# Moving a check flag's load and a branch within the tail of TensorE's product stream

## The chip, the cores and the metric

The kernel runs on one core of one Trainium2 chip. The metric is device time in microseconds (us), the median of several executions. A profile of one execution is shown beside it. Its span, from the first to the last recorded instruction, is about 1.8 us shorter than the time. Ratios are the mean time of one kernel's fast runs over the mean of the other's in the same rounds, so they are not quite the ratio of the medians that are quoted.

## The reference

The reference is attention over a sliding window of a key and value cache, with an input and an output projection, in bfloat16:

```python
B, Sq, D = 8, 32, 1024;  Hq, Hkv, Sk, Dh = 32, 4, 8192, 128
W = min(4096, max(256, Sk // 4))                     # 2048
q = (x @ wq).reshape(B, Sq, Hq, Dh).transpose(0, 2, 1, 3)
k = repeat(k_cache[:, :, Sk - W:, :], Hq // Hkv);  v = the same of v_cache
p = softmax(einsum("bhqd,bhkd->bhqk", q, k) * Dh ** -0.5)
out = einsum("bhqk,bhkd->bhqd", p, v).transpose(0, 2, 1, 3).reshape(B, Sq, Hq * Dh) @ wo
```

## The kernel before

The kernel takes the exponential without first subtracting the row's maximum. That is exact only while the row sums stay in range. So it counts, for each (batch, head group) unit, the rows whose reciprocal sum lies within two limits. If any count is below 128, it branches to a slow, exact fallback. All five engines load the flag into a register and branch. The flag is ready only near the end, so the branch stands in the middle of the last output projection: some products come before it, some after.

```python
            with tc.manual_schedule(engines=order):
                flagi = fast.tail_begin()
        safe = nc.values_load(flagi[0:1, 0:1], min_val=0, max_val=1)     # register load, all engines
        with tc.If(safe < 1, label="fallback"):
            ...                                       # exact attention and projection; clears open PSUM
        with tc.manual_schedule(engines=order):
            fast.tail_end()
    ...
    def tail_begin(self):
        self.pv_last()
        for p in self.after[:-2]: p()
        flagi = self.check_all()                      # count product, minimum, conversion
        for p in self.after[-2:]: p()                 # 4 products of 512 columns
        self.last = self.o_pieces(self.Hkv - 1, 1, (512, 256, 128, 128))
        for p in self.last[:3]: p()                   # a piece is two products (load weights, multiply)
        self.last[3](mm=True)                         # with it: 8 products of 512 columns
        return flagi
    def tail_end(self):
        self.last[3](mm=False)                        # VectorE evicts the 512 columns, DMA to out
        for p in self.last[4:]: p()                   # 8 products of 256, 8 and 8 of 128, each evicted
    def check_all(self):
        ...
        nc.tensor.matmul(cnt[0:1, 0:2 * ncol], lhsT=self.ones_c[:, :], rhs=self.ok[:, :, :], start=True, stop=True)
        low = ck.tile([1, 1], FP32, name="low")
        nc.vector.tensor_reduce(out=low[:, :], in_=cnt[0:1, 0:2 * ncol], op=ALU.min, axis=AX.X)
        flagi = ck.tile([1, 1], I32, name="flagi")
        nc.vector.tensor_scalar(out=flagi[:, :], in0=low[:, :], scalar1=float(P) - 0.5, scalar2=None, op0=ALU.is_ge)
        return flagi
```

Products are summed in PSUM, a memory made of banks. VectorE then *evicts* a group: it adds the sum of the earlier blocks and writes the result to a tile that a DMA copies to the output. The last block's column groups (512, 256, 128, 128) take turns in two PSUM banks. A group may therefore start only when the group two before it has been evicted.

Of the kernel before, what the change touches and what calls it, by code (L numbers as in the profile page):

```python
# [9 lines left out]
ALU = mybir.AluOpType  # L10
AX = mybir.AxisListType
BF16 = mybir.dt.bfloat16
FP32 = mybir.dt.float32
# [20 lines left out]
@with_exitstack  # L34
def kernel(
    ctx: ExitStack,
    tc: tile.TileContext,
    x: bass.AP,
    k_cache: bass.AP,
    v_cache: bass.AP,  # L40
    wq: bass.AP,
    wo: bass.AP,
    out: bass.AP,
):
    nc = tc.nc
    B, Sq, D = x.shape
    _, Hkv, Sk, Dh = k_cache.shape
    HD = wq.shape[1]
    Hq = HD // Dh
    W = min(4096, max(256, Sk // 4))  # L50
    rep = Hq // Hkv
    scale = float(Dh) ** -0.5
    P = 128
    assert Dh == P and D % P == 0 and W % P == 0
    UQ = rep * Sq
    QT_N = UQ // P
    NU = B * Hkv
    out_flat = out.rearrange("b s d -> (b s) d")

    const = ctx.enter_context(tc.tile_pool(name="const", bufs=1))  # L60
    ident = const.tile([P, P], BF16, name="ident")
    make_identity(nc, ident[:, :])
    QT = [const.tile([P, B * UQ], BF16, name=f"QT{g}") for g in range(Hkv)]
    RL_all = const.tile([P, NU * QT_N], FP32, name="RL_all")

    E = mybir.EngineType
    order = {E.PE, E.SP, E.Pool, E.Activation, E.DVE}
    with ExitStack() as long_ctx:
        with ExitStack() as fctx:
            fast = Fast(tc, long_ctx, fctx, x, k_cache, v_cache, wq, wo, out_flat, QT, RL_all, ident)  # L70
            with tc.manual_schedule(engines=order):
                fast.run()
            hint_branch(tc, (E.PE,))
            with tc.manual_schedule(engines=order):
                flagi = fast.tail_begin()
        safe = nc.values_load(flagi[0:1, 0:1], min_val=0, max_val=1)

        with tc.If(safe < 1, label="fallback"):  # L78
            with ExitStack() as ectx:
                eo = ectx.enter_context(tc.tile_pool(name="e_ot", bufs=1))  # L80
                OT_e = eo.tile([P, NU * UQ], BF16, name="OT_e")
                Q_e = eo.tile([P, NU * UQ], BF16, name="Q_e")
                for g in range(Hkv):
                    nc.vector.tensor_copy(out=Q_e[:, g * B * UQ:(g + 1) * B * UQ], in_=QT[g][:, :])
                attention_exact(tc, k_cache, v_cache, Q_e, OT_e, B=B, Hkv=Hkv, Hq=Hq, Sq=Sq, Sk=Sk, W=W, Dh=Dh, scale=scale)
                out_proj(tc, wo, OT_e, out_flat, fast, Hkv=Hkv, Hq=Hq, Sq=Sq, NQ=B * Sq, D=D)

        with tc.manual_schedule(engines=order):
            fast.tail_end()
# [13 lines left out]
class Fast:  # L103
# [4 lines left out]
    def __init__(self, tc, long_ctx, ctx, x, k_cache, v_cache, wq, wo, out_flat, QT, RL_all, ident):  # L108
        self.tc, self.nc, self.ctx = tc, tc.nc, ctx
        self.x, self.k_cache, self.v_cache, self.wq, self.wo, self.out = x, k_cache, v_cache, wq, wo, out_flat  # L110
        self.QT, self.RL_all, self.ident = QT, RL_all, ident
        self.P = P = 128
        self.B, self.Sq, self.D = x.shape
        _, self.Hkv, self.Sk, self.Dh = k_cache.shape
        self.Hq = wq.shape[1] // self.Dh
        self.rep = self.Hq // self.Hkv
        self.W = min(4096, max(256, self.Sk // 4))
        self.NQ = self.B * self.Sq
        self.NT, self.DC, self.KT = self.NQ // P, self.D // P, self.W // P
        self.UQ = self.rep * self.Sq  # L120
        self.QT_N = self.UQ // P
        self.scale = float(self.Dh) ** -0.5
        self.units = [(b, g) for g in range(self.Hkv) for b in range(self.B)]
        self.CJ = 4
        self.NCH = self.KT // self.CJ
        self.VW = self.Dh + 1

        def pool(name, bufs, ctx=ctx, **kw):
            return ctx.enter_context(tc.tile_pool(name=name, bufs=bufs, **kw))

        self.c1 = pool("c1", 1, long_ctx)
        self.wp = pool("wp", 6, long_ctx)
        self.osb = pool("osb", 5, long_ctx)
        self.ps_m = pool("ps_m", 2, long_ctx, space=PSUM)
        self.krp = pool("krp", 4)
        self.kbp = pool("kbp", 2)
        self.kvt = pool("kvt", 2)
        self.ktp = pool("ktp", 5)
        self.vp = pool("vp", 6)
        self.ptp = pool("ptp", 5)  # L140
        self.ob = pool("ob", 2)
        self.ps_s = pool("ps_s", 2, space=PSUM)
        self.ps_o = pool("ps_o", 2, space=PSUM)
        self.OT = self.c1.tile([P, self.Hkv * self.QT_N, 4, self.NQ], BF16, name="OT")
        self.oacc = self.c1.tile([P, self.NT, self.D], FP32, name="oacc")
        self.ok = self.c1.tile([P, 2, len(self.units) * self.QT_N], BF16, name="ok")
        self.ones_c = self.c1.tile([P, 1], BF16, name="ones_c")
        self.xT = self.c1.tile([P, self.DC, self.NQ], BF16, name="xT")
        self.va = [self.c1.tile([P, self.KT, VA_ROW], BF16, name=f"va{i}") for i in range(3)]
        self.wq_t, self.wo_t, self.kT, self.v_sb, self.k_raw = {}, {}, {}, {}, {}  # L150
# [129 lines left out]
    def o_pieces(self, g, t, cuts=(512, 512)):  # L280

        nc, P = self.nc, self.P
        st = {}
        last = g == self.Hkv - 1

        def piece(n0, w, i, mm=None):

            if i == 0:
                st["ps"] = self.open_ps = self.ps_m.tile([P, 512], FP32, name="op_ps", tag="m")
            ps = st["ps"]  # L290
            for k in range(i * 2, i * 2 + 2) if mm is not False else ():
                gq, c = g * self.QT_N + k // 4, k % 4
                nc.tensor.matmul(ps[:, 0:w], lhsT=self.OT[:, gq, c, t * P:(t + 1) * P],  # L293
                                 rhs=self.wo_t[gq][:, c, n0:n0 + w], start=(k == 0), stop=(k == 7))
            if i == 3 and mm is not True:
                acc = self.oacc[:, t, n0:n0 + w]
                if g == 0:
                    nc.vector.tensor_copy(out=acc, in_=ps[:, 0:w])
                elif not last:
                    nc.vector.tensor_tensor(out=acc, in0=ps[:, 0:w], in1=acc, op=ALU.add)  # L300
                else:
                    o_t = self.osb.tile([P, 512], BF16, name="o_t")
                    nc.vector.tensor_tensor(out=o_t[:, 0:w], in0=ps[:, 0:w], in1=acc, op=ALU.add)  # L303
                    eng = nc.sync if n0 in (0, 768) else nc.scalar
                    eng.dma_start(out=self.out[t * P:(t + 1) * P, n0:n0 + w], in_=o_t[:, 0:w])
        return [lambda n0=sum(cuts[:k]), w=w, i=i, **kw: piece(n0, w, i, **kw) for k, w in enumerate(cuts) for i in range(4)]
# [188 lines left out]
    def tail_begin(self):  # L495
        self.pv_last()
        for p in self.after[:-2]:
            p()
        flagi = self.check_all()
        for p in self.after[-2:]:  # L500
            p()
        self.last = self.o_pieces(self.Hkv - 1, 1, (512, 256, 128, 128))
        for p in self.last[:3]:
            p()
        self.last[3](mm=True)
        return flagi

    def tail_end(self):
        self.last[3](mm=False)
        for p in self.last[4:]:  # L510
            p()

    def check_units(self, u0, u1):
# [5 lines left out]
    def check_all(self):  # L519

        nc, P, ck = self.nc, self.P, self.c1
        ncol = len(self.units) * self.QT_N
        cnt = self.ps_o.tile([P, 512], FP32, name="cnt_ps", tag="o_ps")
        nc.tensor.matmul(cnt[0:1, 0:2 * ncol], lhsT=self.ones_c[:, :], rhs=self.ok[:, :, :], start=True, stop=True)
        low = ck.tile([1, 1], FP32, name="low")
        nc.vector.tensor_reduce(out=low[:, :], in_=cnt[0:1, 0:2 * ncol], op=ALU.min, axis=AX.X)
        flagi = ck.tile([1, 1], I32, name="flagi")
        nc.vector.tensor_scalar(out=flagi[:, :], in0=low[:, :], scalar1=float(P) - 0.5, scalar2=None, op0=ALU.is_ge)
        return flagi


def attention_exact(tc, k_cache, v_cache, Q_e, OT_e, *, B, Hkv, Hq, Sq, Sk, W, Dh, scale):
# [55 lines left out]
def out_proj(tc, wo, OT_e, out_flat, fast, *, Hkv, Hq, Sq, NQ, D):  # L588

    nc = tc.nc  # L590
# [6 lines left out]
    with ExitStack() as ctx:  # L597
# [20 lines left out]

        nc.vector.tensor_copy(out=fast.oacc[:, :, :], in_=acc[:, :, :])
        nc.vector.memset(fast.OT[:, (Hkv - 1) * fast.QT_N:, :, :], 0.0)  # L620
        nc.vector.memset(fast.open_ps[:, :], 0.0)


# [28 lines left out]
```

## Time and profile before

| | before |
|---|---|
| time | 186.79 us, median of 3 (186.78 to 186.91) |
| span of the profiled execution | 185.04 us, granted clock 1.0 |
| TensorE busy | 179.5 us, 97% |
| start of the count product to the end of the span ("tail") | 7.952 us |

The page's first part for the kernel before shows busy time, share of the span, and instructions:

```profile
PE 179.5 (97%) x2056; PEld 153.7 (83%) x2072; DVE 115.4 (62%) x268; ACT 131.8 (71%) x133; POOL 94.7 (51%) x150
```

TensorE's stream is what counts. This is the timeline of the kernel before, from 177 us, for TensorE's weight loads (PEld) and products (PE). Its columns are start, duration, engine, line, operation and count, and in brackets the idle time before it and what ended it:

```profile
177.23 0.55 PEld L293 LDWEIGHTS <-OT 128*128 128x128 bf16 x4
177.96 1.54 PEld L293 LDWEIGHTS <-OT 128*128 128x128 bf16 x8 [0.19 <-DVE OT L422]
180.12 1.39 PEld L293 LDWEIGHTS <-OT 128*128 128x128 bf16 x17 [0.61 <-DVEq L78]
181.70 0.43 PEld L293 LDWEIGHTS <-OT 128*128 128x128 bf16 x7 [0.19 <-issue]
...
177.09 0.22 PE L524 MATMUL cnt_ps<-ok,ones_c 128*1 128x128 bf16 x1
177.24 2.76 PE L293 MATMUL op_ps<-wo_sb,OT 128*128 128x512 bf16 x12
180.15 2.15 PE L293 MATMUL op_ps<-wo_sb,OT 128*128 128x256 bf16 x24
```

The products seem to pause for only 0.15 us (177.24+2.76 = 180.00 to 180.15). That understates the gap, because a product is recorded for longer than its slot in the stream. The single records (the trace's own times in ns, which the views round and merge) show that back-to-back 512-column products start every 216 ns and are recorded as 379 ns long. The Trainium skill ("TensorE: Matmul & The Clock Gate", Single matmul latency and Back-to-back issue gap) gives (398+N)/2.4 ns for one product and N/2.4 + 2.5 ns from start to start. For N = 512 that is 379 and 216 ns, so this trace agrees. The second section gives its formula for an isolated product, though. For a stream of load-and-multiply pairs it gives 131 ns at N = 512. This stream is one of such pairs, and it shows 216 ns. The last 512-column product starts at 179.620. The next product could have started at 179.836 and did start at 180.149: **a gap of 0.313 us**.

The next view is the branch's line (L78) in the kernel before, with durations in ns and the times of the first and last start. The engine with a q is that engine's sequencer, the part that loads registers, branches and waits for semaphores (counts by which engines report finished work):

```profile
L78 POOLq COMPARE_BRANCH  x1: 45/45/45, 178.8 to 178.8; - x1
L78 DVEq COMPARE_BRANCH  x1: 72/72/72, 178.9 to 178.9; - x1
L78 PEldq COMPARE_BRANCH  x1: 249/249/249, 178.9 to 178.9; - x1
L78 PEldq EVENT_SEMAPHORE  x1: 51/51/51, 180.0 to 180.0; - x1
```

The last line is the *join*, where the two paths meet again. In the records it starts at 180.042, which is 43 ns after the recorded end of the eighth product (179.999). Its condition is a count on TensorE's own semaphore, and that count arrived at 180.014. In the timeline above, the bracket at 180.12 names VectorE's sequencer (DVEq L78) instead. VectorE's semaphore had last moved at 179.561, well before, so that label does not give the cause.

Last, VectorE in the timeline of the kernel before:

```profile
177.84 0.24 DVE L526 TENSOR_REDUCE low<-cnt_ps 1x1 f32<-1x128 f32 x1
178.11 0.14 DVE L528 TENSOR_SCALAR flagi<-low 1x1 int32<-1x1 f32 x1
178.31 0.69 DVE L303 TENSOR_TENSOR o_t<-op_ps,oacc 128x512 bf16<-128x512 f32 x1
180.04 0.69 DVE L303 TENSOR_TENSOR o_t<-op_ps,oacc 128x512 bf16<-128x512 f32 x1 [1.03 <-PE op_ps L293]
181.22 0.74 DVE L303 TENSOR_TENSOR o_t<-op_ps,oacc 128x256 bf16<-128x256 f32 x2 [0.49 <-PE op_ps L293]
182.34 0.29 DVE L303 TENSOR_TENSOR o_t<-op_ps,oacc 128x128 bf16<-128x128 f32 x1 [0.38 <-PE op_ps L293]
```

The flag takes 0.24 and 0.14 us there. The last eviction, which waits for TensorE, ends 2.4 us before the span does.

### The profile page before, as it was taken

How to read it: one execution, taken by the hardware profiler on the slowest of the kernel's cores; microseconds unless marked ns; L12 is line 12 of the kernel's file. 1: busy time of each engine (PE TensorE's matmuls, PEld its weight loads, DVE VectorE, ACT ScalarE, POOL GpSimd, SP SyncE). 2: the span in 40 equal slices, each digit the busy share in tenths (PEclk: the TensorE clock that was granted, in tenths of full speed). 3: DMA queues.
4: the chain of work that ended last, by engine and by line, in shares of the span. 5: the costliest groups of instructions: out<-in, count | busy, mean ns of one | idle time of the engine just before them, and what ended most of it. 6: DMA issues, size and time to landing. Idle time of an engine off the chain costs nothing. (4 is left out here: it accounts for less than half of the span.)

```text
span 185.0 us, 5079 instructions
## 1 busy us (share of the span) xinstructions
PE 179.5 (97%) x2056; PEld 153.7 (83%) x2072; DVE 115.4 (62%) x268; ACT 131.8 (71%) x133; POOL 94.7 (51%) x150
## 2 busy tenths in 40 slices
PE   7999999999999999999999999999999999999993
PEld 2889999999999999987878999987777888888743
DVE  0138799994586685586467558647745855355372
ACT  2207899786789787878787677787877888888700
POOL 2000008949939959929944980796299289600000
PEclk9999999999999999999999999999999999999999
DMA  5999999998999999999999999999999999980012
GB/s 151 324 391 415 413 414 396 198 231 278 346 332 297 305 329 337 412 215 244 363 357 244 362 386 252 186 342 397 249 381 320 228 288 246 299 131 0 4 58 62
DMA packets 53082, 51.73 MB, mean 280 GB/s; under 512 B 39744, under 2 KB 40256, under 8 KB 53056
## 3 DMA queue, kind: packets, MB, share of 16 engines
q1 hardware_dynamic: 52480, 50.90, 97.8%
q10 hardware_dynamic: 576, 0.49, 0.8%
q8 instruction: 16, 0.26, 0.6%
q14 instruction: 10, 0.08, 0.1%
HBM read 41.42 MB, written 0.52 MB: 227 GB/s over the span
## 5 line engine op out<-in xcount | busy, mean ns | idle before, releaser
L469 ACT ACTIVATE pT<-s_ps 128x1024 bf16<-128x1024 f32 x128 | 128.9, 1025 | 33.3 <-PE s_ps L467 32.3
L259 POOL TENSOR_SCALAR kTv<-kb 32x512 bf16<-32x512 bf16 x140 | 93.7, 670 | 65.1 <-DMA k_raw<-in_k_cache_dram 26.7
L478 PEld LDWEIGHTS <-pT 128*128 128x128 bf16 x1024 | 68.5, 98 | 3.1
L467 PEld LDWEIGHTS <-kT 128*128 128x128 bf16 x368 | 34.8, 98 | 10.3
L293 PE MATMUL op_ps<-wo_sb,OT 128*128 128x512 bf16 (+2 forms) x128 | 33.0, 353 | 0.8
L273 PE MATMUL q_ps<-xT,wq_sb 128*128 128x256 bf16 x192 | 28.1, 273 | 0.0
L478 PE MATMUL o_ps<-va_112,pT 128*128 128x129 bf16 x352 | 27.1, 220 | 0.0
L478 PE MATMUL o_ps<-va_113,pT 128*128 128x129 bf16 x352 | 27.0, 220 | 0.1
L478 PE MATMUL o_ps<-va_114,pT 128*128 128x129 bf16 x320 | 24.7, 220 | 0.0
L249 DVE STREAM_TRANSPOSE kb<-k_raw 128x512 bf16<-128x512 bf16 x36 | 23.8, 684 | 0.0
L415 DVE RECIPROCAL RL_all<-o_ps 128x2 f32<-128x2 f32 x32 | 5.3, 164 | 27.5 <-PE o_ps L478 27.5
L420 DVE TENSOR_SCALAR o_sb<-o_ps,RL_all 128x128 bf16<-128x128 f32 x64 | 19.5, 346 | 1.1
L467 PEld LDWEIGHTS <-kTv 128*128 128x128 bf16 x144 | 13.9, 98 | 5.1
L273 PEld LDWEIGHTS <-wq_sb 128*128 128x128 bf16 x192 | 17.0, 98 | 1.2
L467 PE MATMUL s_ps<-QT_63,kT 128*128 128x256 bf16 x112 | 16.8, 273 | 0.0
L422 DVE STREAM_TRANSPOSE OT<-o_sb 128x256 bf16<-128x256 bf16 x32 | 14.3, 446 | 1.1
L467 PE MATMUL s_ps<-QT_66,kT 128*128 128x256 bf16 x96 | 14.4, 273 | 0.1
L293 PEld LDWEIGHTS <-OT 128*128 128x128 bf16 x144 | 11.3, 98 | 2.9 <-DVEq L78 0.6
L467 PE MATMUL s_ps<-QT_65,kT 128*128 128x256 bf16 x80 | 12.0, 273 | 0.1
L467 PE MATMUL s_ps<-QT_64,kT 128*128 128x256 bf16 x80 | 12.0, 272 | 0.1
L300 DVE TENSOR_TENSOR oacc<-op_ps,oacc 128x512 f32<-128x512 f32 x8 | 5.5, 683 | 7.4 <-PE op_ps L293 7.4
L409 DVE COPY va_113<-v_sb 128x2048 bf16<-128x2048 bf16 x11 | 9.5, 861 | 0.0
(46 smaller groups left out, 105.2 us busy)
## 6 DMA issues: line engine op xcount, KB each, us to landing
v_sb<-in_v_cache_dram SPq DMA_DIRECT2D x29, 512.0 KB, 6.8
wo_sb<-in_wo_dram SPq DMA_DIRECT2D x16, 512.0 KB, 6.8
wq_sb<-in_wq_dram SPq DMA_DIRECT2D x14, 512.0 KB, 7.4
k_raw<-in_k_cache_dram SPq DMA_DIRECT2D x13, 512.0 KB, 6.5
v_sb<-in_v_cache_dram SPq DMA_DIRECT2D x6, 256.0 KB, 5.8
wq_sb<-in_wq_dram SPq DMA_DIRECT2D x4, 256.0 KB, 6.4
kT<-in_k_cache_dram SPq DMA_TRANSPOSE x36, 6.6
k_raw<-in_k_cache_dram SPq DMA_DIRECT2D x2, 256.0 KB, 7.7
```

Source lines behind the costliest of these rows:

```text
L249: nc.vector.transpose(out=st["kb"][:, sl, :], in_=self.k_raw[ui][:, sl, :])
L259: nc.gpsimd.tensor_scalar(out=out, in0=in_, scalar1=1.0, scalar2=1.0, op0=ALU.mult, op1=ALU.mult)
L273: nc.tensor.matmul(st["ps"][:, 0:self.NQ], lhsT=self.wq_t[g, i][:, c % (DC // 2), hl * P:(hl + 1) * P], rhs=self.xT[:, c, :], start=(c == ...
L293: nc.tensor.matmul(ps[:, 0:w], lhsT=self.OT[:, gq, c, t * P:(t + 1) * P], rhs=self.wo_t[gq][:, c, n0:n0 + w], start=(k == 0), stop=(k == 7))
L300: nc.vector.tensor_tensor(out=acc, in0=ps[:, 0:w], in1=acc, op=ALU.add)
L409: self.nc.vector.tensor_copy(out=self.va[ui % 3][:, :, 0:self.Dh], in_=self.v_sb[ui][:, :, :])
L415: nc.vector.reciprocal(out=rl[:, ui * QT_N:(ui + 1) * QT_N], in_=o_ps[:, :, Dh])
L420: nc.vector.tensor_scalar(out=o_sb[:, qt, :, :], in0=o_ps[:, qt, 0:Dh].rearrange("p (i c) -> p c i", c=4), scalar1=rl[:, ui * QT_N + qt:ui ...
L422: nc.vector.transpose(out=self.OT[:, g * QT_N:(g + 1) * QT_N, :, b * self.Sq:(b + 1) * self.Sq], in_=o_sb[:, :, :, :])
L467: nc.tensor.matmul(s_ps[:, jj, :], lhsT=self.kT[ui][:, c * CJ + jj, :], rhs=q_u, start=True, stop=True)
L469: nc.scalar.activation(out=pT[:, :, :], in_=s_ps[:, :, :], func=ACT.Exp, bias=0.0, scale=self.scale)
L478: nc.tensor.matmul(o_ps[:, qt, 0:self.VW], lhsT=pT[:, jj, qt * P:(qt + 1) * P], rhs=va[:, j, 0:self.VW], start=(j == 0 and qt == 0), stop= ...
```

## The change

The intent has two parts. First, get the flag into TensorE's register sooner: the minimum is written as an integer, which saves the conversion, and it is loaded when only four of the last eight products have been issued. Second, put four of the 256-column products ahead of the branch, so that the array has work while TensorE's sequencer branches. The core of the diff:

```diff
-                flagi = fast.tail_begin()
-        safe = nc.values_load(flagi[0:1, 0:1], min_val=0, max_val=1)
-        with tc.If(safe < 1, label="fallback"):
+                low = fast.tail_begin()
+                safe = nc.values_load(low[0:1, 0:1], min_val=0, max_val=P)
+                fast.tail_mid()
+        with tc.If(safe < P, label="fallback"):
 ...
-        for p in self.last[:3]:
+        for p in self.last[:2]:
             p()
+        return low
+    def tail_mid(self):
+        self.last[2]()
         self.last[3](mm=True)
-        return flagi
+        for p in self.last[4:6]:
+            p()
     def tail_end(self):
         self.last[3](mm=False)
-        for p in self.last[4:]:
+        for p in self.last[6:]:
 ...
-        low = ck.tile([1, 1], FP32, name="low")
+        low = ck.tile([1, 1], I32, name="low")
         nc.vector.tensor_reduce(out=low[:, :], in_=cnt[0:1, 0:2 * ncol], op=ALU.min, axis=AX.X)
-        flagi = ...
+        return low
 ...
-        nc.vector.memset(fast.open_ps[:, :], 0.0)      # fallback: clear the open bank
+        for ps in fast.open_ps:                        # now the last two open banks
+            nc.vector.memset(ps[:, :], 0.0)
```

More of the change, by code (lines that the diff above doesn't have):

```diff
@@ L147, in __init__ @@
         self.ones_c = self.c1.tile([P, 1], BF16, name="ones_c")
+        self.open_ps = []
         self.xT = self.c1.tile([P, self.DC, self.NQ], BF16, name="xT")
@@ L288, in piece @@
             if i == 0:
-                st["ps"] = self.open_ps = self.ps_m.tile([P, 512], FP32, name="op_ps", tag="m")
-            ps = st["ps"]
+                st[n0] = self.ps_m.tile([P, 512], FP32, name="op_ps", tag="m")
+            ps = st[n0]
+            self.open_ps = ([q for q in self.open_ps if q is not ps] + [ps])[-2:]
             for k in range(i * 2, i * 2 + 2) if mm is not False else ():
@@ L498, in tail_begin @@
             p()
-        flagi = self.check_all()
+        low = self.check_all()
         for p in self.after[-2:]:
@@ L524, in check_all @@
         nc.tensor.matmul(cnt[0:1, 0:2 * ncol], lhsT=self.ones_c[:, :], rhs=self.ok[:, :, :], start=True, stop=True)
-        low = ck.tile([1, 1], FP32, name="low")
+        low = ck.tile([1, 1], I32, name="low")
         nc.vector.tensor_reduce(out=low[:, :], in_=cnt[0:1, 0:2 * ncol], op=ALU.min, axis=AX.X)
-        flagi = ck.tile([1, 1], I32, name="flagi")
-        nc.vector.tensor_scalar(out=flagi[:, :], in0=low[:, :], scalar1=float(P) - 0.5, scalar2=None, op0=ALU.is_ge)
-        return flagi
+        return low
 def attention_exact(tc, k_cache, v_cache, Q_e, OT_e, *, B, Hkv, Hq, Sq, Sk, W, Dh, scale):
```

## The prediction

> **What bounds the kernel now.** TensorE is busy 97% of the 185.0 us span (page, part 1) at granted clock 1.0; the time is its stream of products plus a tail. The change touches only the last 8 us. In the timeline from 177 us TensorE runs twelve 512-column output products (one starts every 216 ns, the last at 179.62), then eight 256-column (108 ns apart) and sixteen 128-column ones (55 ns apart). The chain of waits at the end is: products, VectorE's eviction, products, last eviction (182.34 to 182.63), then output DMA and closing barriers, 2.4 us that the change leaves alone.
>
> **Where the flag costs today.** The views of the flag and of the If's line give: reduction 177.84 to 178.07, conversion 178.11 to 178.25, register load on TensorE's sequencer 178.29 to 178.78 (0.49 us), compare-and-branch 178.95 to 179.19 (249 ns). Seven products were queued behind the running one when the load began, so neither load nor branch starved the array. The Trainium skill ("Advanced Engine Details and Errata", Control Flow Timing) gives about 108 ns for a compare-and-branch; this trace has 45 to 72 ns on the other engines and 249 ns here. The real cost is the semaphore instruction where the paths join: it starts at 180.04, because it waits for TensorE's *own* semaphore, 43 ns after the eighth product's end at 180.00. That product had its columns in at 179.62+0.216 = 179.84; the next one starts at 180.15. So the join costs a bubble of about 0.31 us: 0.16 us of pipeline tail, the rest semaphore and restart. It is on the critical path.
>
> **What the change does.**
> - Removes the conversion (0.142 us) and moves the load up by about 0.18 us. Not critical: the branch was ready before the drain.
> - Puts the load after four of eight products. It would run from about 178.11 to 178.60; queued products last to 178.97. Resuming costs up to 0.17 us (today's gap from load to branch), so no bubble.
> - Issues eight products between load and branch. Estimate from today's 24 products between join and closing drain (1.6 us): 66 ns each, so the branch starts near 179.4 and ends by 179.65. The other engines show 0.35 to 0.52 us from branch to join, so TensorE could be there near 180.1.
> - Puts four 256-column products (432 ns) behind the last 512-column one. They would cover the bubble if the join still waited only for the 512-column one: about 0.31 us won, and the later evictions shift with it.
> - But the fallback must wait for those four too (it clears their PSUM tile), and the join waits for everything ahead of the branch. I expect the wait to move with the branch, to the fourth 256-column product. Its tail is as long: 270-108 = 162 ns against 379-216 = 163 ns. Then the bubble is moved, not removed: the join starts near 180.47, the next product at 180.58, and the evictions after it are where they were.
>
> I give the moved bubble 75%, the covered one 25%.
>
> **Prediction.** 186.72 us, range 186.40 to 186.92 (covered: about 186.48; moved: 186.79). Faster by over 2%: 0.005; within 2%: 0.99; slower: 0.005.
>
> **What would show it.** Right: in TensorE's timeline a gap of about 0.3 us after four 256-column products instead of before them, the join starting about 40 ns after the fourth one's end, last eviction still at 182.34. Wrong: products every 216 or 108 ns through the branch, last eviction near 182.03.
>
> **What would make it wrong.** The early load holds the sequencer until the array runs dry near 178.97; or the branch, now later, is no longer hidden.

## The result, and the profile after

| | before | changed |
|---|---|---|
| time, median of 6 | 186.93 us (186.78 to 187.02) | 187.12 us (186.37 to 187.31) |
| ratio of fast runs | | 1.0004 (95%: 0.9986 to 1.0021) |
| span of the profiled execution | 185.04 us | 185.41 us |
| tail | 7.952 us | 7.954 us |

The time is the same within noise. The median of 187.12 lies above the predicted range, which ended at 186.92.

The timeline of the changed kernel, TensorE's loads and products from the count product on:

```profile
177.60 0.55 PEld L296 LDWEIGHTS <-OT 128*128 128x128 bf16 x4
178.33 2.19 PEld L296 LDWEIGHTS <-OT 128*128 128x128 bf16 x12 [0.18 <-DVE OT L425]
180.92 0.95 PEld L296 LDWEIGHTS <-OT 128*128 128x128 bf16 x13 [0.40 <-issue]
182.06 0.43 PEld L296 LDWEIGHTS <-OT 128*128 128x128 bf16 x7 [0.19 <-issue]
...
177.45 0.22 PE L532 MATMUL cnt_ps<-ok,ones_c 128*1 128x128 bf16 x1
177.60 5.07 PE L296 MATMUL op_ps<-wo_sb,OT 128*128 128x512 bf16 x36
```

All 36 products now print as one piece of 5.07 us, as if the pause were gone. It is not gone. The loads' line still has an idle stretch, now after the twelfth product, and the single records have the fourth 256-column product at 180.529 and the fifth at 180.951. At 108 ns from start to start, the fifth was due at 180.637: **a gap of 0.314 us**. The recorded ends of neighbouring products overlap or nearly meet, so the merged line hides a gap of this size. Starts tell the truth here, and busy time does not. The Trainium skill ("Perfetto Trace Analysis", Summary: the profiler window per engine type) says that a TensorE record ends at an estimated end, which fits the records here: nearly every 512-column product at full clock is 379 or 380 ns long. No run shows where the true ends lie.

The branch's line in the changed kernel (L79), TensorE's sequencer:

```profile
L79 PEldq COMPARE_BRANCH  x1: 253/253/253, 179.4 to 179.4; - x1
L79 PEldq EVENT_SEMAPHORE  x1: 51/51/51, 180.8 to 180.8; - x1
```

In the records the join starts at 180.844, 42 ns after the fourth 256-column product's recorded end (180.802). VectorE at the end of the changed kernel's timeline:

```profile
178.20 0.24 DVE L534 TENSOR_REDUCE low<-cnt_ps 1x1 int32<-1x128 f32 x1
178.68 0.69 DVE L306 TENSOR_TENSOR o_t<-op_ps,oacc 128x512 bf16<-128x512 f32 x1 [0.24 <-PE op_ps L296]
180.40 0.69 DVE L306 TENSOR_TENSOR o_t<-op_ps,oacc 128x512 bf16<-128x512 f32 x1 [1.04 <-PE op_ps L296]
181.59 0.74 DVE L306 TENSOR_TENSOR o_t<-op_ps,oacc 128x256 bf16<-128x256 f32 x2 [0.49 <-PE op_ps L296]
182.71 0.29 DVE L306 TENSOR_TENSOR o_t<-op_ps,oacc 128x128 bf16<-128x128 f32 x1 [0.38 <-PE op_ps L296]
```

The conversion is gone, and everything else stands 0.36 to 0.37 us later than before. So does the count product, which comes before any changed instruction (177.45 against 177.09). Counted from that product, the last eviction starts at 5.254 us here and at 5.256 us before. The 0.37 us therefore arises earlier, in code that is the same in both kernels.

The table cuts each execution with a trace into three parts. The *head* runs from the start of the span to the first exponential, the *middle* from there to the count product, and the *tail* is the rest:

| execution | head | middle | tail | span |
|---|---|---|---|---|
| before | 13.96 | 163.12 | 7.95 | 185.04 |
| changed | 14.28 | 163.18 | 7.95 | 185.41 |

The head makes 0.31 us of the 0.37. The experiments had to answer two questions: whether the moved bubble explains the tail, and whether the head differs by chance.

### The profile page after: what moved, and what is told of

The parts are those of the page before. It is cut to its first block, busy times and chain, and to the rows that moved or that the text cites. A ratio compares the mean times of both kernels' runs of the same rounds, so it can differ in the third digit from the quotient of the medians.

```text
span 185.4 us, 5095 instructions
## 1 busy us (share of the span) xinstructions
PE 180.8 (97%) x2072; PEld 154.1 (83%) x2072; DVE 115.4 (62%) x267; ACT 131.9 (71%) x133; POOL 95.3 (51%) x150
## 5 line engine op out<-in xcount | busy, mean ns | idle before, releaser
L296 PE MATMUL op_ps<-wo_sb,OT 128*128 128x512 bf16 (+2 forms) x144 | 36.5, 355 | 0.2
```

The costliest lines, as they stand in the source:

```text
L296: nc.tensor.matmul(ps[:, 0:w], lhsT=self.OT[:, gq, c, t * P:(t + 1) * P], rhs=self.wo_t[gq][:, c, n0:n0 + w], start=(k == 0), stop=(k == 7))
```

## The experiments

Two theories of the tail stood against each other. Theory: the join waits until all of TensorE's products ahead of it are complete, so the gap goes wherever the branch goes, while load, conversion and branch are hidden. Rival: the gap is a cost of the load, of the branch, or of the change from one group to the next. Tails are read from one trace each. In the executions whose edits leave the tail's timing alone they agree within about 0.01 us, except for one run whose closing waits took longer, noted below (experiment 9).

### 1. Integer flag and early load alone

The edit to the changed kernel takes the four more products back behind the branch:

```diff
-        for p in self.last[4:6]:
-            p()
 ...
-        for p in self.last[6:]:
+        for p in self.last[4:]:
```

> Integer flag and early load alone; the branch stays directly behind the eight 512-column products. Tail below means from the start of the count product to the end of the span: 7.952 us in the kernel before, 7.954 us in the changed one. Theory (the load is hidden, the join's drain is what costs): tail 7.95 within 0.03, the gap of 0.31 us on TensorE ahead of the first 256-column product as in the kernel before. Rival (the 0.14 us conversion and the later load lay on the path): tail 7.77 to 7.85.

The tail was 7.943 us. The gap of 0.312 us stood ahead of the first 256-column product, as before the change, and the join was at 2.956 us after the count product, as it was before. The time, one run, was 187.15 us beside 186.68 us for the kernel before. The early load is worth nothing, so the rival's 7.77 to 7.85 falls.

### 2. Four more products ahead of the branch alone

The flag is made in two steps again and loaded after all the products ahead of the branch:

```diff
-                low = fast.tail_begin()
-                safe = nc.values_load(low[0:1, 0:1], min_val=0, max_val=P)
-                fast.tail_mid()
+                flagi = fast.tail_begin()
+                fast.tail_mid()
+        safe = nc.values_load(flagi[0:1, 0:1], min_val=0, max_val=1)
```

> Four more products ahead of the branch alone; flag made in two steps and loaded after all products, as before. Theory (the join waits for everything ahead of the branch, so the bubble only moves): tail 7.95 within 0.03, gap of 0.31 us after the fourth 256-column product, join 0.04 us after that product's end. Rival (the four products cover the bubble, and in the changed kernel the early load took the gain back): tail 7.64, no gap over 0.1 us.

The tail was 7.952 us, with a gap of 0.313 us after the fourth 256-column product and the join at 3.392 us (changed kernel: 3.391). The time was 187.23 us, one run. The load's place makes no difference, and the four products do not cover the gap. They move it.

### 3. The load with too little ahead of it

The load goes ahead of all eight products of the last block:

```diff
-        for p in self.last[:2]:
-            p()
         return low
     def tail_mid(self):
-        self.last[2]()
+        for p in self.last[:3]:
+            p()
```

> As the changed kernel, but the load stands ahead of all eight products of the last block; only the count product and four products are ahead of it. Theory (the load holds back everything behind it on TensorE, and is free only while earlier products are queued): the array runs dry about 1.02 us after the count product, load over at 1.50, first product behind it at 1.56 to 1.67; tail 8.50 to 8.60. Rival (products behind the load go on while it waits): tail 7.95.

The timeline of this run shows the hole (the view ends at 180 us, so its second line has seven of the eight products):

```profile
177.21 1.04 PE L296 MATMUL op_ps<-wo_sb,OT 128*128 128x512 bf16 x4
178.60 1.67 PE L296 MATMUL op_ps<-wo_sb,OT 128*128 128x512 bf16 x7 [0.35 <-issue]
```

Its register load on TensorE's sequencer:

```profile
L76 PEldq TENSOR_LOAD <-low x1: 492/492/492, 178.1 to 178.1; - x1
```

In the records the load runs from 178.083 to 178.575, and the first product behind it starts 26 ns later. From start to start that is a gap of 0.516 us, and the tail is 8.467 us. The mechanism is the expected one, but the cost is slightly below the expected 0.55 to 0.65, because TensorE resumed in 26 ns and not in 60 to 170. The time, one run, was 187.30 us beside 186.68. A register load does hold back everything behind it on TensorE. In both main kernels it is free because products ahead of it were still waiting to start when it began: seven in the kernel before, four in the changed one. Here all four had started.

### 4. A third PSUM bank

In the last block, TensorE also waits 0.23 us for a bank ahead of the last group (181.465 to 181.697 in the trace before, from the same start-to-start arithmetic; the 256-column eviction that frees the bank ends at 181.645). One of the two banks of the attention output is idle by then. It gets a pool of its own that lives on through the branch, and the cuts become three:

```diff
+        self.ps_a = pool("ps_a", 1, long_ctx, space=PSUM)
-        self.ps_o = pool("ps_o", 2, space=PSUM)
+        self.ps_b = pool("ps_b", 1, space=PSUM)
 ...                    # units take ps_a and ps_b in turn; the last cut of the last block takes ps_a
-        self.last = self.o_pieces(self.Hkv - 1, 1, (512, 256, 128, 128))
+        self.last, self.open_ps = self.o_pieces(self.Hkv - 1, 1, (512, 256, 256)), []
```

> As the changed kernel, but a third PSUM bank for the last block (one of the attention's two, which is idle then), cut 512, 256, 256 in place of 512, 256, 128, 128; the branch where the changed kernel has it. Theory: the wait for a bank ahead of the last group (0.23 us) goes, the join's gap of 0.31 us stays; last eviction starts about 5.00 us after the count product, tail 7.83 (7.77 to 7.88).

TensorE's loads from the last block on, in two pieces with the join's pause between them:

```profile
178.57 2.19 PEld L299 LDWEIGHTS <-OT 128*128 128x128 bf16 x12 [0.18 <-DVE OT L428]
181.16 1.22 PEld L299 LDWEIGHTS <-OT 128*128 128x128 bf16 x12 [0.40 <-issue]
```

The last eviction started at 5.005 us, as expected, and the join's gap was 0.313 us. The tail was 7.937 and not 7.83 (7.77 to 7.88). The 0.23 us on TensorE was given back: the last eviction, of 256 columns, takes 425 ns instead of 291, and the last output DMA and closing waits took 2.51 us after it instead of 2.41. The records split these 0.10 us: the last DMA lands 1.55 us after the eviction's end instead of 1.51, and SyncE, which checks the DMAs one after another, has one more check (0.06 us) to make after it. The time, one run, was 187.44 us beside 186.68.

### 5. The third bank, with nothing on TensorE behind the branch

All products go ahead of TensorE's branch. VectorE's evictions stay behind its own branch:

```diff
-        for p in self.last[4:6]:
-            p()
+        for p in self.last[4:7]:
+            p()
+        self.last[7](mm=True)
+        for p in self.last[8:11]:
+            p()
+        self.last[11](mm=True)
 ...
-        for p in self.last[6:]:
-            p()
+        for k in (7, 11):
+            self.last[k](mm=False)
```

> As the run with a third PSUM bank, but every product stands ahead of TensorE's branch, so nothing on TensorE is behind the join. Theory (the 0.31 us gap is the join's wait for its own products to drain): no gap over 0.05 us, last eviction starts 4.69 us after the count product instead of 5.005, tail 7.62 (7.58 to 7.66) against 7.937. Rival (the gap comes from the change from one output group to the next, or from the bank, not from the join): gap still there, tail 7.93.

The timeline of this run, TensorE's loads and the last evictions:

```profile
178.34 3.50 PEld L298 LDWEIGHTS <-OT 128*128 128x128 bf16 x24 [0.18 <-DVE OT L427]
...
181.29 0.42 DVE L308 TENSOR_TENSOR o_t<-op_ps,oacc 128x256 bf16<-128x256 f32 x1 [0.18 <-PE op_ps L298]
182.16 0.42 DVE L308 TENSOR_TENSOR o_t<-op_ps,oacc 128x256 bf16<-128x256 f32 x1 [0.45 <-PE op_ps L298]
```

All 24 loads of the last block run in one piece, and no gap is left between product starts. The join starts at 4.703 us, when all products are done and nothing waits for it. The last eviction starts at 4.697 us instead of 5.005. The tail is 7.632 us, 0.305 us less than in experiment 4, for one edit: the products of the same cuts in the same banks moved across the branch. The gap belongs to the join. Nor is it the time that a branch takes: in all 13 traces the join starts 42 or 43 ns after the recorded end of the last product ahead of it, while from the end of TensorE's branch to the join it is anything from 0.57 us (experiment 2) to 2.11 us (here). No run takes the wait itself out of the join. The time was 186.78 us (186.40 to 186.87, 6 runs) beside 186.96, ratio 0.9987 (0.9970 to 1.0005).

### 6. A version meant to beat both

As experiment 5, with cuts 512, 320, 192 (the last cut still takes the third bank), and the last block's output DMAs on the other queue each, so that the last one is on ScalarE's. The core of the edit:

```diff
-self.o_pieces(self.Hkv - 1, 1, (512, 256, 256))
+self.o_pieces(self.Hkv - 1, 1, (512, 320, 192))
```

> A version meant to beat both: as the run before it, cuts 512, 320, 192 and the last output DMA on the other queue. Theory: last eviction starts at 4.70 us after the count product, lasts about 0.36 us; tail 7.47 (7.42 to 7.55), 0.48 us under both kernels; time ratio to the kernel before 0.9974 (0.9960 to 0.9990). Rival (the end is bound by something else, the DMA or the closing barriers): tail 7.9, ratio 1.000.

The last eviction started at 4.696 us and took 358 ns, as expected. The tail was 7.564 us, slightly more than the expected 7.55 at most. The close after the eviction took 2.51 us as in experiment 5, so the other queue did not bring it back to the 2.41 of the kernel before. The time was 187.05 us (186.45 to 188.61, 6 runs), ratio 1.0015 (0.9980 to 1.0051), not the 0.9960 to 0.9990 expected. One run of 188.61 us raises this mean; the other five average 186.86 us, beside 186.89 for the kernel before.

### 7 and 8. Both kernels again, unchanged

> The kernel before, unchanged, against itself. Theory (executions differ by when the first weight pieces land, within the first 14 us; nothing after): single times spread over about 0.9 us; span less the start of the first exponential is 171.08 within 0.1 as in the trace of before; ratio 1.000. Rival (the kernel before is steady, within 0.25 us, and only the changed kernel has a spread, of its own making): spread under 0.3 us.

> The changed kernel, unchanged. Theory (the change is worth nothing: the bubble moved): ratio 1.000, interval within 0.9990 to 1.0010; tail 7.95 within 0.02; same spread of single times as the unchanged kernel in the same rounds. Rival (the change costs or wins something in the early part): ratio clear of 1 by over 0.0005.

The kernel before, against itself on the same chip, gave 186.87 us (186.64 to 187.41, 6 runs), ratio 1.0001 (0.9981 to 1.0020). Its runs beside it in the same rounds went from 186.50 to 187.46, apart from one run of 484.11 us that is not counted as fast and not explained. So the kernel before spreads as widely as the changed one, and the calm of its first runs (0.13 us over three) was luck, as far as these sets can tell. The rival, that only the changed kernel has a spread, falls. The changed kernel gave 186.82 us (186.51 to 187.44, 6 runs), ratio 0.9998 (0.9978 to 1.0019). The interval is twice as wide as hoped for, but it is centred on no change, and the tail was 7.953 us.

The parts of all other executions with a trace:

| execution | head | middle | tail |
|---|---|---|---|
| before, again | 14.05 | 163.13 | 7.95 |
| changed, again | 14.47 | 163.13 | 7.95 |
| load alone | 14.30 | 163.13 | 7.94 |
| four products alone | 14.36 | 163.13 | 7.95 |
| load too early | 13.76 | 163.30 | 8.47 |
| third bank | 14.57 | 163.13 | 7.94 |
| third bank, all ahead | 14.34 | 163.13 | 7.63 |
| third bank, all ahead, second set | 13.81 | 163.29 | 7.63 |
| cuts 512, 320, 192 | 14.59 | 163.14 | 7.56 |
| cuts 512, 320, 192, second set | 13.98 | 163.38 | 7.56 |
| fewer first weights (experiment 9) | 13.72 | 163.13 | 8.06 |

The head is the part that wanders: from 13.76 to 14.59 us, by 0.83, in the executions whose code for it is unchanged (all but experiment 9). The middle, 163 us of dense work, is 163.12 to 163.18 us in all but three. Those three (163.29, 163.30 and 163.38) are among the four lowest of these heads, so part of an early start was lost again. Why is open.

### 9. What the head waits for

In the head, TensorE waits for the first weights and keys to arrive. These are the waits of its weight loads from 5 to 14.5 us in the kernel before, in the third-bank run, and in the kernel before run again: engine, line, what it waited for, us in total, times, longest.

```profile
PEld L375 <- DMA wq_sb<-in_wq_dram: 0.9, 2, 0.5
PEld L368 <- DMA k_raw<-in_k_cache_dram: 0.2, 1, 0.2
```

```profile
PEld L381 <- DMA wq_sb<-in_wq_dram: 1.6, 2, 1.2
PEld L374 <- DMA k_raw<-in_k_cache_dram: 0.2, 1, 0.2
```

```profile
PEld L375 <- DMA wq_sb<-in_wq_dram: 1.5, 3, 1.1
```

The edit takes the last two of the first weights' pieces (0.5 MB) out of the kernel before:

```diff
-        wq0 = self.load_wq(0, 0, (1, 1, 2)) + self.load_wq(0, 1, (2, 1, 1))
+        wq0 = self.load_wq(0, 0, (1, 1, 2)) + self.load_wq(0, 1, (2,))
-        wq0[4]()
-        wq0[5]()
```

> The kernel before without the last two 256 KB pieces of the first weights (the products use two earlier pieces again, so the result is wrong on purpose). Theory (the first exponential, and with it the whole time, waits for the first weights and keys to arrive): in ten traces the first exponential starts at 13.76 to 14.59 us; with 0.5 MB less ahead of the keys, at about 400 GB/s, it starts at 12.7 to 13.4; tail 7.95 as ever. Rival (the start is set by when TensorE's full clock is granted, 5.3 to 7.0 us in those traces): 13.7 to 14.6, unchanged.

The head was 13.72 us: the lowest of all, but not the 12.7 to 13.4 expected, and inside the rival's range. So this run does not by itself decide between the two. Its later waits for weights and keys are gone, and from the seventeenth product of the first projection (8.60 us, still held up by a weight piece) to the first exponential it took 5.12 us. Exactly 5.12 us stands in two other executions too (the kernel before again, and cuts 512, 320, 192 in their second set), and 5.46 to 5.96 us in the other ten. In the three with 5.12 us, TensorE's loads wait for no DMA after that product. TensorE's own work thus sets a floor that the expectation left out. Above it lie the waits for pieces of weights and keys. Why these pieces land earlier in one execution than in another stays open.

The rival, the grant of the full clock, does not order the heads. The latest head of 14.59 had the grant at 5.33 us, one of the earlier ones, and 7.04 us went with 14.36. (The trace of experiment 3 has no grant on record.) Yet the two earliest grants (4.23 and 4.41) went with low heads (13.81 and 13.98), so a share of the clock in the head is not excluded. The output passed the comparison with the reference although its first query projection used wrong weights, so that comparison says little about this kernel. Its tail of 8.06 has the last eviction at the usual 5.257 us. The last DMA landed no later than usual (1.49 us after the eviction's end), but SyncE then had two more checks of other DMAs to make, 0.12 us. The time, one run, was 186.68 us.

### 10 and 11. The two better tails once more

> The version meant to beat both, once more, for a closer ratio (its first set held one run of 188.61 us). Theory: tail 7.56, 0.39 us under the kernel before; the start-up spreads as before; ratio about 0.9979 and below 1 in its interval. Rival (its start-up is slower): ratio over 1.000.

> Third bank, all products ahead of TensorE's branch, once more. Theory: tail 7.63, 0.32 us under the kernel before; ratio about 0.9983 (first set 0.9987).

The cuts 512, 320, 192 gave 186.62 us (186.26 to 188.06, 6 runs) beside 186.90, ratio 0.9996 (0.9969 to 1.0023). Again one run stood out high, and why this version has one in each set is open. The third bank with all products ahead gave 186.78 us (186.51 to 187.07, 5 runs), ratio 0.9995 (0.9982 to 1.0008). Both tails repeated (7.558 and 7.630 us). Both sets of experiments 5 and 11 together give a mean of 186.73 us over 11 runs, against 186.92 us over the 21 fast runs beside them. That is 0.19 us less, with a standard error of about 0.08 worked out from the two spreads. The traces show 0.32 us less in the tail; no single set shows it clear of the head's wandering. The pool is made of sets on two chips. Neither forecast ratio came: 0.9979 with an interval below 1, and 0.9983.

## Why the prediction was right or wrong

- **The moved bubble (given 75%): right.** The prediction placed the join near 180.47 and the next product at 180.58. The changed kernel's trace is 0.367 us late at the count product; with that taken off, they stand at 180.477 and 180.584. The gap measured 0.314 us against 0.313 before.
- **The covered bubble (25%): wrong.** Experiment 2 showed it alone. Experiment 5 showed what does remove the gap, which is to leave nothing on TensorE behind the branch.
- **Load and conversion not critical: right.** Experiment 1 gave 7.943 against 7.952 us. The load moved up by 0.18 us, as predicted (1.021 after the count product against 1.200).
- **No bubble at the load: right.** Experiment 3 showed that the danger named was real, and cost 0.52 us with four products fewer ahead.
- **The branch's start near 179.4: wrong by about 0.34 us, without effect.** With the offset taken off, it started at 179.06. The estimate of 66 ns per issued product was too high: 8 products and the branch's own delay took 0.47 us. The lower figure of 0.35 us from branch to join was too low as well; the records give 0.41 to 0.52 on the other engines.
- **The range: wrong, and this is the step that failed.** "186.72 us, range 186.40 to 186.92" took both the level of the kernel before, 186.79 us, and its noise from three runs, 0.13 us apart, and pulled the centre down by 0.07 us for the covered case. What stands in its place: in the six runs of the comparison the kernel before had a median of 186.93 us itself, already above the range. Single runs of the unchanged kernel go from 186.50 to 187.46 us, and the traced heads differ by 0.83 us where their code is unchanged. A median of six such runs can miss a range of 0.52 us without any effect of the change. It was 187.12 in the first set and 186.82, inside the range, in the second; with a level near 186.9 us, which side of 186.92 a set falls on is largely chance.

## What to carry to other kernels

When an engine has work on both sides of a branch, look at what the join waits for. Here it was completion of that engine's own work, so extra work ahead of the branch moved a 0.31 us gap and did not fill it; only leaving that engine nothing to do behind the branch removed it. Judge such gaps by instruction starts, because merged busy time showed the gap in one kernel and hid it in the other. Before giving a range of a few tenths of a microsecond, learn the spread of the unchanged kernel from many runs, and compare the changed part from a marker inside the trace.

## What the Trainium skill lacked or had wrong

- No page states what a path join costs: TensorE waited for its own semaphore, 0.313 us from when the next product was due to its start; 0.16 us of that is by how much the last product's record outlasts its slot (379 against 216 ns).
- "Runtime: NRT & Kernel Launch" (Instruction fetch mechanics) gives about 200 ns per register for a register load. The loads here, of one value each from SBUF, took 469 to 543 ns on the five engines of the kernel before.
- "Advanced Engine Details and Errata" (Control Flow Timing) gives about 108 ns for a compare-and-branch. Here it was 45 to 72 ns on four engines and 249 to 266 ns on TensorE's sequencer.
- No page gives the time from the end of such a branch to the next recorded instruction, the join's: 0.41 to 0.52 us on the four other engines of the kernel before. That may include a wait; no run separates the two.
- "TensorE: Matmul & The Clock Gate" was right to the nanosecond with its formulas for product lengths and spacing (379 and 216 ns for 512 columns). Its figures for a stream of load-and-multiply pairs, 131 ns at 512 columns and 81 ns at 128, did not fit: this stream of such pairs shows 216 and 55 to 56 ns. The page does not say that a register load on TensorE's sequencer stops the products behind it; experiment 3 has 0.52 us for that.
